# A fused recurrent-attention and MoE kernel: scalar loads further back on GpSimd, three loads split, and a new order of loads and work

## The chip, the cores and the metric

The kernel runs on one core of a Trainium2 chip. The metric is the time of one execution on the device in microseconds (us). The kernel before took 186.28 us, the median of 13 runs (184.48 to 188.73).

A core has five engines, each with an instruction queue of its own that runs in order: TensorE (PE, matrix products; its weight loads are listed as PEld), VectorE (DVE), ScalarE (ACT), GpSimd (POOL) and SyncE (SP, which here only issues DMAs). The queues meet at semaphores. An instruction that waits holds back all that stand behind it on its queue.

## The reference

Two parts follow each other. The first is a gated linear recurrence over 768 steps for 4 batches of 8 heads, with head size 48:

```python
for t in range(S):
    state = alpha[:, :, t, :, None] * state + np.einsum('bhd,bhe->bhde', k[:, :, t], v[:, :, t])
    y[:, :, t] = np.einsum('bhd,bhde->bhe', q[:, :, t], state)
```

Its output, put together to x of 3072 tokens by 384, goes through one layer with a hidden size of 2048:

```python
h = x @ w_in
r = np.maximum(h, 0.0)
g = s * (r * r) + b
return (g @ w_out).astype(np.float32)
```

The scalars s and b are single numbers. Inputs and output are float32.

## The kernel before

**Blocks.** The 3072 tokens are 24 blocks of 128 (6 to a batch). Within a block the recurrence is written as matrix products. ACT takes the logarithm of alpha (`st_ln`, L381); PE sums it over time with a triangular matrix (`st_cum`, L387, and L394 for the sum over the block); ACT takes the exponential of the sums and of their negatives (L403, L406, L408); DVE multiplies q and k with these (L417, L422); POOL casts v (L411). The scaled q and k are needed transposed: ACT issues a DMA transpose for that (`st_Tdma`, L439). PE then forms the key-value product for the state (L448) and the scores (`st_A`, L490), DVE masks the scores (L499) and updates the state (L469, L473; POOL L484 multiplies with the block's decay), PE forms y (L528), and ACT copies y to bf16 (L673).

**Pairs.** The first four blocks are loaded and worked two by two ("pairs" 0 and 1, L551 to L661), with PE in place of the DMA transposes (L605, copied out by DVE at L616). Half of a pair's values have to change their place among the partitions: POOL casts them (L621), PE moves them (`pair_vshift`, L631), and `pair_vcopy` (L644) copies them out of PSUM, on the engine that `VC2` names.

**The layer.** Finished blocks are put into groups of one or two (`GROUPS`, L18). For each group the first product is done in units of 512 output columns in PSUM (`mm1`, L693): six matmuls of 256 columns for a group of two blocks, twelve of 128 for a single one. There are 96 units. ACT applies the ReLU (L702) and DVE squares (L708). The second product (`mm2`, L755) is done in quads of four matmuls, four quads to a block; DVE scales it with s and adds the bias (L766), and SP stores it (L779). The bias row is b times the column sums of w_out: DVE adds these up (L343, L348, L351), multiplies ones with b (L363), and one matmul (L368) makes the row. The eight weight pieces, called i0 to i3 and o0 to o3, come in float32 and are cast to bf16 by the engines in `CE` (L319 on ACT, L321 on DVE, L323 on POOL).

**What sets the order.** A planner (class `Schedule`, L55 to L143) takes all operations with an engine, a cost, a priority and what they read and write. It runs through them with its own clock, gives each engine the ready operation of lowest priority value, and writes out the instructions in the order found. Priorities are a block's due time `want(n)` (from `UNIT` and `LEAD`) plus an offset for the kind of operation (the table `P`). Costs, such as `TC` for the casts, also only affect the order. Where the planner sees PE idle before the first `mm2`, it puts filler matmuls on zeros (L1028). The order of the first loads on SP is the list `LOADS`: capitals stand for pairs, small letters for single blocks. Later loads come in the order of their blocks, and a load waits until its one of five buffers is free. Stores stand on the same SP queue. One store, of block `STQ` = 18, is issued by POOL.

**Places that the change touches.** The scalar loads (`load_bs`, L358 to L360, planned at L847) stand on POOL behind the setup memsets and ahead of the first value casts of pair 0. `load` (L223 to L228) issues one DMA for one tensor of one block. `NKV` says from which block on the key-value product uses another PSUM bank, `NPE` up to which block PE would transpose a single block; since the first four blocks are pairs, that is none.

Of the kernel before, what the change touches and what calls it, by code (L numbers as in the profile page):

```python
# [14 lines left out]

VW = 144

GROUPS = [2, 2, 1, 1, 1, 1, 2, 2, 2, 2, 2, 2, 2, 2]  # L18
UNIT = 0.392
LEAD = {1: 204.6, 2: 323.1, 4: 100.0}  # L20

NPE = 4

NAY = 12

# [6 lines left out]
TP = 1.45  # L32
LATE = 2.5
NY = 2
NKV = 7
NR2 = 2
STQ = 18
TC2 = ["DVE", "DVE"]
VC2 = ["ACT", "ACT"]
CE = ["POOL", "DVE", "ACT", "ACT", "ACT", "ACT", "ACT", "ACT"]  # L40
TC = dict(ACT=1.4, DVE=0.87, POOL=2.0)
FILL_GAP = 0.2
COLD = 9.0

P_BM, P_CS, P_BMM = -5, -286.4, 473.5
P = dict(
    ln=34.88, cum=-15.29, eb=-32.24, ei=9.49, vc=73.43, qb=-9.65, kb=14.71, T=95.62,
    Tc=-13.62, KV=-13.54, t1=9.55, sn=124.73, Ay=-11.39, A=-22.53, mk=-58.68, y=-13.83,
    ye=5.65, m1=-19.67, re=9.86, sq=-33.02, m2=-18.25, oe=-24.3, vm=-57.17, ci=324.52,
    co=-825.8, ls=148.33, vn=-450.01,  # L50
)

LOADS = ["V0", "i0", "A0", "K0", "Q0", "A1", "V1", "Q1", "i1", "K1", "i2", "i3", "v4", "o0", "o1", "o2", "o3", "a4", "k4", "q4"]

class Schedule:  # L55
    HOP = 0.05
# [90 lines left out]
def kernel(  # L147
# [12 lines left out]
    nc = tc.nc  # L160
    ctx.enter_context(tc.manual_schedule())

    B, H, S, D = q.shape
    C = 128
# [7 lines left out]
    NIN = 5  # L172
# [31 lines left out]
    a_in = many("a_in", NIN, [128, H, D], FP32)  # L204
# [17 lines left out]

    def load(n, src, dst):  # L223
        b, c = n // NCH, n % NCH
        nc.sync.dma_start(
            out=dst[n % NIN],
            in_=src[b, :, c * C : (c + 1) * C, :].rearrange("h s d -> s h d"),
        )  # L228

    for x, src in enumerate((alpha, q, k, v)):  # L230
        load_pair(0, x, src)
# [62 lines left out]
    out_sb = many("o_sb", 3, [128, d_model], FP32)  # L294
# [368 lines left out]
    blk_group = []  # L663
    for g, m in enumerate(GROUPS):
        blk_group += [(g, t) for t in range(m)]
# [11 lines left out]
    quads = []  # L677
    for g, m in enumerate(GROUPS):
        per = 4 // m
        for u in range(NJ // per):  # L680
            units.append((g, [u * per + i for i in range(per)]))
        for tt in range(m):
            for jq in range(NJ // 4):
                quads.append((g, tt, jq))
    first_blk = [sum(GROUPS[:g]) for g in range(len(GROUPS))]

    def mm1(w):
        g, js = units[w]
        n = GROUPS[g] * C
        hp = h_ps[w % 2]  # L690
# [84 lines left out]
    def ostore(x):  # L775
        g, tt, jq = quads[x]
        n = first_blk[g] + tt
        eng = nc.gpsimd if n == STQ else nc.sync
        eng.dma_start(out=out[n * C : (n + 1) * C, :], in_=out_sb[(x // 4) % 3])  # L779


    sched = Schedule()
    op = sched.op
    NG = len(GROUPS)

# [31 lines left out]
    for rank, item in enumerate(loads):  # L817
        t, i = rank - 1000, int(item[1:])
        if item[0] in "AQKV":
            if i == 1:  # L820
                load_pair_op(item[0], i)
            continue
        if item[0] in "aqkv":
            if i < N1 + NIN:
                load_op(item[0], i)
            continue
        st = stage
        stage += 1
        key = [("wst", st)]
        if st >= NST:  # L830
            h = (st - NST) // 2 % 2
            key = [("gt", x, j) for x in range(9 - 3 * h, 12 - 3 * h) for j in range(NJ)]
            key = key[24 * (st % 2) : 24 * (st % 2) + 24] + [("wst", st)]
        if st >= NST:
            reuse.append((len(sched.ops), [(x, h) for x in ("AQ", "KV")[st % 2]]))
        eng = CE[st]
        if item[0] == "i":
            op("SP", TW, t, load_w_in, i, st, w=key, lat=2.0)
            op(eng, TC[eng], P["ci"], cast_w_in, i, st, eng, r=key, w=[("wib", i)], lock=eng != "ACT")
        else:  # L840
            op("SP", TW, t, load_w_out, i, st, w=key, lat=2.0)
            op(eng, TC[eng], P["co"], cast_w_out, i, st, eng, r=key, w=[("wob", i)], lock=eng != "ACT")
            op("DVE", 0.88, P_CS, colsum_part, i, st, r=key,
               w=["colpart" if i else "colsum"], lock=True)
            if i:
                op("DVE", 0.88, P_CS, colsum_add, r=["colpart"], w=["colsum"], lock=True)
    op("POOL", 1.3, P["ls"], load_bs, w=["b", "s"], lat=3.5)  # L847
    op("DVE", 0.3, P_BM, bias_mul, r=["b"], w=["bones"], lock=True)
    op("DVE", 0.44, P_CS, colsum_fold, w=["colsum"], lock=True)
    ys = {}  # L850
# [4 lines left out]
    def pb(n):  # L855
        return "ct" if n >= NKV else "py"

# [106 lines left out]
    def add_group(g):  # L964
        nonlocal unit_i, quad_i
        if g == 0:
            op("PE", 0.65, P_BMM, bias_mm, r=["bones", "colsum"], w=[("o", 0)], lat=0.16)
            op("DVE", 0.53, -300, bias_copy, r=[("o", 0)], w=["bias"])
        m = GROUPS[g]
        ring = [(first_blk[g] + x) % RING for x in range(m)]  # L970
        per = 4 // m
        for u in range(NJ // per):
            w = unit_i
            unit_i += 1
            js = units[w][1]
            t = w * UNIT
            op("PE", {1: 0.67, 2: 0.656, 4: 0.648}[m], t + P["m1"], mm1, w,
               r=[("xd", g % 3, x) for x in range(m)] + [("wib", js[0] // 4)],
               w=[("h", w % 2)], lat=0.16)
            op("ACT", 0.52, t + P["re"], relu, w, r=[("h", w % 2)], w=[("r", w % 2)])  # L980
            op("DVE", 0.345, t + P["sq"], square, w, r=[("r", w % 2)],
               w=[("gt", x, j) for j in js for x in ring], lock=True)
        for u in range(4 * m):
            x = quad_i
            quad_i += 1
            tt, jq = quads[x][1:]
            if x >= len(quads) - 4:
                continue
            ob = (x // 4) % 2
            t = (x + 4 * m + P["m2"]) * UNIT  # L990
            op("PE", 0.65, t, mm2, x,
               r=[("gt", ring[tt], j) for j in range(4 * jq, 4 * jq + 4)] + [("wob", jq)],
               w=[("o", ob)], lat=0.16)
# [69 lines left out]
```

## Time and profile before

| what | value |
|---|---|
| median of 13 runs | 186.28 us |
| the profiled execution: time, span in the profile | 186.5 us, 184.7 us |
| mean granted clock of PE | 0.982 |
| PE, PEld busy | 173.6, 123.8 us |
| DVE, ACT, POOL busy | 133.4, 105.7, 39.9 us |
| first products L693 | 73.2 us in 672 matmuls |
| second products L755 | 68.9 us in 368 matmuls |
| ReLU L702, square L708 | 55.3 and 42.4 us, 96 each |
| HBM read, written | 25.17 MB, 4.72 MB |
| DMA transposes, issue to landing | 20, 2.9 to 6.8 us, median 5.3 |
| loads of 192 KB, issue to landing | 4.7 to 4.8 us at the median |

The span runs from the first to the last instruction; the execution's time is 1.8 us longer. Busy times leave out the instructions that only issue DMAs, so an ACT that is issuing a transpose does not show as busy. Matmuls are pipelined, and their ends are modelled: their starts are the safer thing to read. The chain that ended last is found by going back from the last instruction, at each step to what released it; "issue" in it is time for which the profile shows no reason.

### The profile page before, as it was taken

The page shows a single profiled execution, that of the slowest core. Times are in us where ns is not written, and L with a number is a line of the kernel's source. Part 1 is how long each engine was busy: PE and PEld are TensorE (multiplying, and loading weights), DVE is VectorE, ACT ScalarE, POOL GpSimd, SP SyncE. Part 2 cuts the span into 40 slices and gives each one's busy share as a digit, 9 for nine tenths or more (in the row PEclk, how much of TensorE's full clock was granted, in tenths as well). Part 3 has the DMA queues.
Part 4 walks back from the last instruction along what each step waited for, and adds up shares of the span by engine and source line. Part 5 has one row for each costly group of instructions (what it writes and reads, how often), then busy time and mean ns, then how long its engine had stood idle before and what let it go on. Part 6 is the DMA issues. An engine that isn't in the chain of part 4 may idle for free.

```text
span 184.7 us, 5347 instructions
## 1 busy us (share of the span) xinstructions
PE 173.6 (94%) x2151; PEld 123.8 (67%) x2151; DVE 133.4 (72%) x251; ACT 105.7 (57%) x215; POOL 39.9 (22%) x71
## 2 busy tenths in 40 slices
PE   6689996999999999999989999999999799999993
PEld 2345774756778677766667776787767577777662
DVE  2477799999497887759769996878778586553321
ACT  3434899956646565685357674685657355665000
POOL 7994032021013311211203230111212130010000
PEclk9975999999999999999999999999999999999999
DMA  5999999999999999999999999999986892000122
GB/s 154 357 272 386 349 372 282 181 174 239 248 191 225 188 149 282 178 209 222 229 192 229 178 217 229 197 192 170 215 173 137 154 173 77 0 19 28 56 76 85
DMA packets 119961, 35.48 MB, mean 192 GB/s; under 512 B 113232, under 2 KB 118352, under 8 KB 119936
## 3 DMA queue, kind: packets, MB, share of 16 engines
q1 hardware_dynamic: 98688, 29.70, 70.9%
q10 hardware_dynamic: 21120, 5.25, 22.0%
q8 instruction: 17, 0.28, 0.6%
q0 software_dynamic: 128, 0.20, 0.3%
q14 instruction: 8, 0.07, 0.1%
HBM read 25.17 MB, written 4.72 MB: 162 GB/s over the span
## 4 chain that ended last, share of the span: by engine, by line
PE 64%; DVE 12%; DMA 10%; POOL 5%; issue 3%; ACT 3%; ACTq 1%; SPq 0%; POOLq 0%; DVEq 0%
PE o_ps L755 25%; PE h_ps L693 24%; DMA qkT<-qk 7%; PE py_ps L528 4%; PE a_ps L490 3%; DMA v_in<-in_v_dram 3%; DVE gt L708 2%; DVE colpart L343 2%; ACT r L702 2%; DVE colsum L348 2%; DVE am L499 2%; PE ct_ps L387 1%; DVE s_st L473 1%; PE o_ps L1028 1%; PE o_ps L724 1%
## 5 line engine op out<-in xcount | busy, mean ns | idle before, releaser
L693 PE MATMUL h_ps<-xd,w_in_bf 128*128 128x256 bf16 (+1 forms) x672 | 73.2, 257 | 0.7 <-ACT r L702 0.6
L702 ACT ACTIVATE r<-h_ps 128x512 bf16<-128x512 f32 x96 | 55.3, 601 | 29.7 <-PE h_ps L693 10.4
L755 PE MATMUL o_ps<-w_out_bf,gt 128*128 128x384 bf16 x368 | 68.9, 326 | 1.4 <-ACT w_out_bf L319 1.3
L693 PEld LDWEIGHTS <-w_in_bf 128*128 128x128 bf16 x672 | 56.2, 98 | 10.5 <-issue 1.0
L708 DVE TENSOR_TENSOR gt<-r 128x512 bf16<-128x512 bf16 x96 | 42.4, 456 | 15.2 <-ACT r L702 14.8
L755 PEld LDWEIGHTS <-gt 128*128 128x128 bf16 x368 | 34.3, 98 | 20.3 <-issue 1.5
L499 DVE TENSOR_TENSOR am<-a_ps,mask 128x1024 bf16<-128x1024 f32 x24 | 29.3, 1221 | 3.2 <-PE a_ps L490 3.0
L411 POOL CAST vp<-v_in 128x384 bf16<-128x384 f32 x20 | 12.0, 600 | 61.3 <-DMA v_in<-in_v_dram 48.4
L484 POOL TENSOR_TENSOR s_st<-s_st,blast 128x384 bf16<-128x384 bf16 x16 | 14.0, 874 | 49.0 <-DVE s_st L473 29.2
L766 DVE SCALAR_TENSOR_TENSOR o_sb<-o_ps,s_col,bias_w 128x384 f32<-128x384 f32 x23 | 14.2, 615 | 8.8 <-PE o_ps L755 8.4
L673 ACT ACTIVATE xd<-py_ps 128x384 bf16<-128x384 f32 x22 | 11.1, 504 | 11.9 <-PE py_ps L528 11.8
L381 ACT ACTIVATE la<-a_in 128x384 bf16<-128x384 f32 x20 | 10.5, 527 | 7.0 <-DMA a_in<-in_alpha_dram 3.5
L417 DVE TENSOR_TENSOR qk<-q_in,b_s 128x384 bf16<-128x384 f32 x20 | 11.9, 597 | 2.6 <-ACT b_s L403 2.5
L473 DVE TENSOR_TENSOR s_st<-ct_ps,s_st 64x192 bf16<-64x192 f32 x24 | 8.5, 354 | 6.5 <-PE ct_ps L448 5.4
L403 ACT ACTIVATE b_s<-ct_ps 128x384 f32<-128x384 f32 x20 | 9.8, 491 | 5.7 <-PE ct_ps L394 3.3
L422 DVE TENSOR_TENSOR qk<-k_in,binv 128x384 bf16<-128x384 f32 x20 | 11.0, 549 | 0.9 <-DMA k_in<-in_k_dram 0.8
L490 PEld LDWEIGHTS <-qkT 64*128 64x128 bf16 x192 | 5.6, 95 | 6.8 <-issue 5.1
L490 PE MATMUL a_ps<-qkT 64*128 64x128 bf16 x192 | 9.8, 222 | 0.4 <-DMA qkT<-qk 0.2
L406 ACT ACTIVATE binv<-ct_ps 128x384 f32<-128x384 f32 x20 | 9.9, 494 | 0.0
L1028 PE MATMUL o_ps<-zeros 128*128 128x512 bf16 x21 | 7.6, 495 | 1.3 <-DVE zeros L236 1.3
L528 PE MATMUL py_ps<-am,vp 128*32 128x128 bf16 x352 | 8.8, 219 | 0.0
L528 PEld LDWEIGHTS <-vp 128*32 128x32 bf16 x384 | 6.8, 100 | 0.5 <-issue 0.2
(93 smaller groups left out, 125.5 us busy)
## 6 DMA issues: line engine op xcount, KB each, us to landing
out_dram<-o_sb SPq DMA_DIRECT2D x22, 192.0 KB, 2.9
v_in<-in_v_dram SPq DMA_DIRECT2D x20, 192.0 KB, 4.8
a_in<-in_alpha_dram SPq DMA_DIRECT2D x20, 192.0 KB, 4.8
k_in<-in_k_dram SPq DMA_DIRECT2D x20, 192.0 KB, 4.7
q_in<-in_q_dram SPq DMA_DIRECT2D x20, 192.0 KB, 4.7
wst<-in_moe_w_in_dram SPq DMA_DIRECT2D x4, 768.0 KB, 8.0
gt<-in_moe_w_out_dram SPq DMA_DIRECT2D x4, 768.0 KB, 9.5
gt<-in_alpha_dram SPq DMA_DIRECT2D x2, 384.0 KB, 4.6
```

What stands on the lines that cost most here:

```text
L411: nc.gpsimd.tensor_copy(out=vp_sb[n % 4].rearrange("a p (x d) -> a p x d", d=D)[:, :, 0:3:2, :], in_=v_in[n % NIN].rearrange("a (p e) d -> ...
L417: nc.vector.tensor_tensor(out=qk_sb[n % 4][:, 0, :, 0:D], in0=q_in[n % NIN], in1=b_sb[n % 2], op=ALU.mult)
L484: nc.gpsimd.tensor_tensor(out=s_sb[n % 3], in0=t1_sb[n % 2], in1=bl, op=ALU.mult)
L490: nc.tensor.matmul(out=a_ps[:, e, p, :], lhsT=qkT[64 * e : 64 * e + 64, 1, p, :], rhs=qkT[64 * e : 64 * e + 64, 0, p, :], start=True, stop ...
L499: nc.vector.tensor_tensor(out=am_sb[n % 2].rearrange("a e p t -> a (e p) t"), in0=a_ps.rearrange("a e p t -> a (e p) t"), in1=(mask2 if n ...
L528: nc.tensor.matmul(out=y_of(n)[32 * (x % 4) : 32 * (x % 4) + 32, x // 4, :], lhsT=(st[:, p, c0 : c0 + 32] if e is None else vp[:, p, c0 + ...
L673: nc.scalar.activation(out=dst, in_=src, func=AF.Copy)
L693: nc.tensor.matmul(out=hp[:, i * n : (i + 1) * n], lhsT=w_in_bf[:, kk, 128 * j : 128 * (j + 1)], rhs=xd_sb[g % 3][:, kk, 0:n], start=(kk = ...
L702: nc.scalar.activation(out=r_sb[w % 2], in_=h_ps[w % 2], func=AF.Relu)
L708: nc.vector.tensor_tensor(out=gt_sb[:, s0 : s0 + m, js[0] : js[0] + len(js)].rearrange("a s j t -> a j s t"), in0=r, in1=r, op=ALU.mult,)
L755: nc.tensor.matmul(out=op[:, 0:d_model], lhsT=gt_sb[:, s0, j], rhs=w_out_bf[:, j, :], start=(j == 0), stop=(j == NJ - 1),)
L766: nc.vector.scalar_tensor_tensor(out=ots, in0=o_ps[(x // 4) % 2][:, 0:d_model], scalar=s_col, in1=bias_w, op0=ALU.mult, op1=ALU.add,)
```

## The change

Seven things change. The first is a new dependence, which makes the planner put the scalar loads behind the arrival of pair 1's values. The second splits three loads (q, k and v of block 20) into two DMAs of four heads each. Third, the store of block 18 goes to SP. Fourth, `VC2` puts one of the two value copies of each pair on DVE. Fifth, the groups change: nine of two blocks and six of one, instead of ten and four. Sixth, `LOADS` has a new order. Seventh, the planner gets other due times, offsets, costs and port rules, so that the order of the instructions changes on every engine. `NKV` goes from 7 to 6.

```diff
-GROUPS = [2, 2, 1, 1, 1, 1, 2, 2, 2, 2, 2, 2, 2, 2]
-UNIT = 0.392
-LEAD = {1: 204.6, 2: 323.1, 4: 100.0}
-NPE = 4
+GROUPS = [2, 1, 1, 1, 2, 2, 2, 1, 2, 2, 1, 2, 2, 1, 2]
+UNIT = 0.92
+LEAD = {1: 111.4, 2: 111.7, 4: 19.2}
+NPE = 3
...
-NKV = 7
+NKV = 6
-STQ = 18
-VC2 = ["ACT", "ACT"]
+VC2 = ["DVE", "ACT"]
-TC = dict(ACT=1.4, DVE=0.87, POOL=2.0)
+TC = dict(ACT=1.43, DVE=1.7, POOL=1.44)
...
-LOADS = ["V0", "i0", "A0", "K0", "Q0", "A1", "V1", "Q1", "i1", "K1", "i2", "i3", "v4", "o0", "o1", "o2", "o3", "a4", "k4", "q4"]
+LOADS = ["i0", "A0", "V0", "A1", "V1", "i1", "K0", "Q0", "Q1", "K1", "v4", "i2", "i3", "o0", "o1", "q4", "o2", "o3", "a4", "k4"]
...
     def load(n, src, dst):
         b, c = n // NCH, n % NCH
-        nc.sync.dma_start(
-            out=dst[n % NIN],
-            in_=src[b, :, c * C : (c + 1) * C, :].rearrange("h s d -> s h d"),
-        )
+        parts = 2 if n == 20 and dst is not a_in else 1
+        for x in range(parts):
+            hs = slice(H // parts * x, H // parts * (x + 1))
+            nc.sync.dma_start(
+                out=dst[n % NIN][:, hs],
+                in_=src[b, hs, c * C : (c + 1) * C, :].rearrange("h s d -> s h d"),
+            )
...
-        eng = nc.gpsimd if n == STQ else nc.sync
-        eng.dma_start(out=out[n * C : (n + 1) * C, :], in_=out_sb[(x // 4) % 3])
+        nc.sync.dma_start(out=out[n * C : (n + 1) * C, :], in_=out_sb[(x // 4) % 3])
...
-    op("POOL", 1.3, P["ls"], load_bs, w=["b", "s"], lat=3.5)
+    op("POOL", 1.3, P["ls"], load_bs, r=[("V", 1)], w=["b", "s"], lat=3.5)
```

All entries of `P` change as well (for the scalar loads, ls goes from 148.33 to 233.89), and the casts of weights and two costs of matmuls in the planner. How the order comes out: on POOL the two scalar loads stand behind pair 1's casts and the state update of block 1, and ahead of block 4's value cast; before, they were the first thing behind the memsets. On DVE the value copies stand behind pair 0's copies of transposes (L616) and behind block 1's mask, and the bias multiply L363 moves from behind block 1's mask to behind pair 1's copies of transposes. On PE there are 51 matmuls more: 48 of the first product and three fillers. On SP the store of block 15, which stood ahead of block 22's k and v loads, stands behind all loads.

More of the change, by code (lines that the diff above doesn't have):

```diff
@@ L34 @@
 NY = 2
-NKV = 7
+NKV = 6
 NR2 = 2
-STQ = 18
 TC2 = ["DVE", "DVE"]
-VC2 = ["ACT", "ACT"]
+VC2 = ["DVE", "ACT"]
 CE = ["POOL", "DVE", "ACT", "ACT", "ACT", "ACT", "ACT", "ACT"]
-TC = dict(ACT=1.4, DVE=0.87, POOL=2.0)
+TC = dict(ACT=1.43, DVE=1.7, POOL=1.44)
 FILL_GAP = 0.2
 COLD = 9.0
-P_BM, P_CS, P_BMM = -5, -286.4, 473.5
+P_BM, P_CS, P_BMM = -5, -217.4, 512.0
 P = dict(
[L47 to L50, printed above, removed]
+    ln=50.93, cum=-11.7, eb=-25.98, ei=-14.28, vc=58.17, qb=19.99, kb=-17.0, T=38.45,
+    Tc=-30.89, KV=-13.93, t1=-24.57, sn=118.3, Ay=-40.59, A=-32.64, mk=-45.84, y=-19.88,
+    ye=10.8, m1=-10.02, re=0.24, sq=-21.45, m2=-8.17, oe=-41.19, vm=-66.4, ci=345.81,
+    co=-1666.27, ls=233.89, vn=70.38,
 )
-LOADS = ["V0", "i0", "A0", "K0", "Q0", "A1", "V1", "Q1", "i1", "K1", "i2", "i3", "v4", "o0", "o1", "o2", "o3", "a4", "k4", "q4"]
+LOADS = ["i0", "A0", "V0", "A1", "V1", "i1", "K0", "Q0", "Q1", "K1", "v4", "i2", "i3", "o0", "o1", "q4", "o2", "o3", "a4", "k4"]
 class Schedule:
@@ L838 @@
             op("SP", TW, t, load_w_in, i, st, w=key, lat=2.0)
-            op(eng, TC[eng], P["ci"], cast_w_in, i, st, eng, r=key, w=[("wib", i)], lock=eng != "ACT")
+            op(eng, TC[eng], P["ci"], cast_w_in, i, st, eng, r=key, w=[("wib", i)], lock=eng == "POOL")
         else:
             op("SP", TW, t, load_w_out, i, st, w=key, lat=2.0)
-            op(eng, TC[eng], P["co"], cast_w_out, i, st, eng, r=key, w=[("wob", i)], lock=eng != "ACT")
+            op(eng, TC[eng], P["co"], cast_w_out, i, st, eng, r=key, w=[("wob", i)], lock=eng == "POOL")
             op("DVE", 0.88, P_CS, colsum_part, i, st, r=key,
@@ L976, in add_group @@
             t = w * UNIT
-            op("PE", {1: 0.67, 2: 0.656, 4: 0.648}[m], t + P["m1"], mm1, w,
+            op("PE", {1: 0.675, 2: 0.66, 4: 0.652}[m], t + P["m1"], mm1, w,
                r=[("xd", g % 3, x) for x in range(m)] + [("wib", js[0] // 4)],
@@ L990, in add_group @@
             t = (x + 4 * m + P["m2"]) * UNIT
-            op("PE", 0.65, t, mm2, x,
+            op("PE", 0.655, t, mm2, x,
                r=[("gt", ring[tt], j) for j in range(4 * jq, 4 * jq + 4)] + [("wob", jq)],
```

## The prediction

> **What bounds the kernel now.** I read the page first (shares of the span, the 40 slices), then the windows by stage, then the chain that ended last, then the waits, and the timeline only where these pointed.
>
> ```profile
> span 184.7 us, 5347 instructions
> ...
> PE 173.6 (94%) x2151; PEld 123.8 (67%) x2151; DVE 133.4 (72%) x251; ACT 105.7 (57%) x215; POOL 39.9 (22%) x71
> ...
> PEclk9975999999999999999999999999999999999999
> ```
>
> TensorE is busy nearly throughout, and the only half-speed stretch lies in slices 2 and 3 (about 9 to 18.5 us). The windows view splits this into stages:
>
> ```profile
> 10.00:15.00 5.00, 4.31 (x49) 2.11 (x52) 3.34 (x8) 1.70 (x3) 4.64 (x8) 0.68 1.08 297
> ...
> 30.00:35.00 5.00, 4.15 (x52) 3.29 (x41) 4.97 (x8) 5.00 (x6) 0.78 (x1) 1.00 0.86 180
> ...
> 40.00:50.00 10.00, 10.00 (x125) 6.68 (x124) 7.43 (x16) 6.61 (x16) 1.47 (x2) 1.00 1.24 229
> ```
>
> The columns after the length are PE, PEld, DVE, ACT, POOL busy, then clock and DMA. There are three stages. Up to 19.5 us a latency chain runs through POOL, PE and DVE. From 19.5 to 38 us DVE (18.03 of 18.50 busy) and ACT (17.77) are full, and the bias matmul at 38.04 waits for DVE's column sums. From 38 us on PE is full. So time can be won in three ways only: an earlier start of the second stage, a shorter second stage, or fewer stalls of PE in the third.
>
> The chain shows where the first stage hangs:
>
> ```profile
> 8.21 0.63 POOL b_col L359
> 8.84 0.54 POOL s_col L360
> 9.38 0.52 POOL vc L621
> ...
> 10.52 0.51 POOL vp L621
> 11.07 0.41 PE py_ps L655 x6
> 11.70 0.35 DVE s_st L469
> ```
>
> The two scalar loads stand on POOL ahead of the value casts, and these ahead of the first key-value matmuls. The values had landed at 7.81 (their issue at 3.00 plus 4.81), so the loads hold the chain.
>
> In the third stage the same view shows the largest stall:
>
> ```profile
> 139.38 0.63 DVE o_sb L766
> ...
> 140.02 0.36 SPq L779
> ...
> 140.43 0.43 SPq L225
> ...
> 140.95 5.00 DMA v_in<-in_v_dram
> ...
> 146.07 0.51 POOL vp L411
> ...
> 146.63 0.33 PE ct_ps L448 x4
> ```
>
> A store on SP waits for its output tile; behind it stand block 22's k and v loads; the value lands 5.00 us after its issue, is cast, and PE has stood 1.09 us (start of the matmul less start and usual 0.16 us of the one before). Measured in this way, starts against usual starts, the stalls over 0.2 us after 40 us are 0.21 at 61.4, 0.36 at 70.4, 0.80 at 96.3, 0.26 at 108.4 and 1.09 at 146.6: 2.7 us in all. Two are named in the waits:
>
> ```profile
> PE ct_ps L448 <- POOL vp L411: 0.9, 1, 0.9
> PE h_ps L693 <- ACT r L702: 0.6, 1, 0.6
> ```
>
> **Part by part.** Line numbers are those of before.
>
> *Scalar loads (L359, L360) behind the second pair's values.* POOL's first cast starts at 8.21 instead of 9.38, so 1.17 us earlier. What is late next? The two pair transposes on PE end at 9.77, so the first shift matmul gains little (9.94 to about 9.8), the second goes from 10.51 to about 10.0, and the first key-value matmuls from 11.07 to about 10.2, when the third cast is done. Then DVE is late: its second copy of transposes ends at 10.65 either way, and the change puts a value copy there (L644, 0.49 on ACT), so the state operation starts at about 11.15 instead of 11.70. The mask follows at 11.9 (was 12.47), the next score matmuls at 13.5 (were 14.21), the first y at 14.05 (14.76). One more filler matmul ahead of the second y costs 0.43 at half clock, of which about 0.15 shows; y starts at 15.5 (16.08), and the pair's scaling on DVE, which opens the full stretch, at about 19.0 instead of 19.53. Gain: 0.55. The floor is 0, if DVE or the fillers eat it; the ceiling 1.17.
>
> *The loads' new place.* They issue after the first state update, at about 14.6 instead of 8.16, and landed 4.3 us later at the longest, so at about 19. The bias multiply (L363, 0.28) moves from a gap at 16.01 to behind the pair's transposes, at about 23. That hides the landing with 4 us to spare. But its 0.28 now lies in the full DVE stretch: a loss of 0.28. The Trainium skill, page "SBUF — State Buffer", section "SBUF: two separate sides", speaks against this place: a DMA issued by GpSimd cannot have its descriptors written while VectorE holds the shared port, and the next section tells of 620 ns grown to 3100 ns. By that page I estimate two such delays, 5 us, and then a stall of about 1 us at the bias multiply and a sum 1 us worse; no row here shows it, since both loads ran while VectorE had gaps.
>
> *Value copies on DVE, one per pair.* Both fall where DVE waited (1.05 before 11.70, 1.30 before 19.53); the first is in the chain above, the second costs nothing.
>
> *Load order.* i1 goes ahead of Q1, v4 ahead of i2, q4 ahead of o2. Transfers land one behind the other here (192 KB in 0.5 to 0.9 us), so o3 lands at about 33.0 instead of 32.41. Its first user on DVE ran at 35.24; even 0.5 earlier it is covered by 1.7. Nothing.
>
> *Groups.* Nine groups of two blocks and six of one replace ten and four. One pair of blocks more is done by 96 matmuls of 128 columns instead of 48 of 256. Twelve of the first kind take as long as six of the second: the chain has 24 of the first kind in 1.34 at 48.14 and 12 of the second in 1.33 at 81.06. Eight units at 0.01: 0.1 loss.
>
> *Three late loads (q, k, v of block 20) split in two.* Three more issues on SP, 0.4 to 0.8 each. SP stands still from 126.4 to 127.95 just behind them. Nothing, at most 0.3.
>
> *Store of block 18 from POOL to SP.* SP then does it among the last stores; nothing waits behind it but stores. Nothing.
>
> *New order of SP.* I counted PE's work (0.665 a unit of first matmuls, 0.65 a quad of second ones, 0.34 scores, 0.56 y) between the end of the block whose store stands just ahead of a load and that load's use. Before, the shortest are k22 3.5 us, k7 5.5, k11 5.7, k15 6.2; after, k7 7.0, a22 7.4, k14 8.0. A load took 4.7 to 4.8 at the median from issue to landing. So the stall at 146.6 goes (1.09), and so does the one at 108.4 (0.26), whose k15 was scaled 0.7 late for that reason. What is late next there is a22: 7.4 us against about 6 needed. Gain 1.35; bounds 0.7 to 1.4.
>
> *New order of PE, ACT and DVE.* Three distances matter. First, from a block's cumulative sum to its scores lie exponentials, scaling and a DMA transpose of 2.9 to 6.8 us (median 5.3). It gets shorter in 14 of 20 blocks: 13.1 to 10.9 for block 7, 9.9 to 8.4 for 11, 8.8 to 8.0 for 8, 8.2 to 7.5 for 23. With the transposes of before, block 9 stalls 0.3 again and 5, 7, 13 come within 0.7 of it; I put 0.6 against the 0.36 of before: loss 0.25. Second, the stall at 96.3 is ACT's: a transpose issue held it 2.18 instead of 1.27, and the next first matmul had 0.5 us to spare. The shortest such reserve is 0.67 after, and three were under it before: gain 0.5 of the 0.8. Third, DVE: between a first matmul and the one that needs its buffer again stand a ReLU (0.60), a square (0.46) and what DVE has queued ahead; in two units (29 and 60) 0.2 us are left over there, where none had under 0.8: loss 0.4, up to 1.
>
> Sum: -0.55 + 0.28 + 0.1 - 1.35 + 0.25 - 0.5 + 0.4 = -1.4. The profiled execution took 186.5 (its span and 1.8 around it), which is 0.2 over the median 186.28. So 185.1 in its terms and **184.9** in those of the median.
>
> **Rivals.** *The stalls only move (186.1).* The load stalls end, but PE is full, and the tighter transposes and squares take it back: 0.55 gained, 0.38 lost (0.28 + 0.1), and 1.85 (1.35 and 0.5) offset by 1.8. For it: DVE works 15 to 17 of each 20 us in the third stage and convoys move easily. Against: the load stalls have a named cause that goes. This is also the case in which the change does not do what it says, since the scalar loads' own part is then worth 0.2.
>
> *The transposes become the bound, on the other side (188.1).* If each takes 1 us longer than before, because the loads that now stand ahead of the stores share the DMA engines with them, blocks 4 to 16 have -0.3 (5), -0.7 (7), -0.2 (8), -1.3 (9), -0.4 (11), -0.6 (13), -0.3 (16) to spare: a loss of 3.8 in place of 0.6, so 3.2 over the forecast, 188.1. The point from which it costs more than the rest gains is about 0.45 us more per transpose (1.4 of 3.2), a mean of 5.5 instead of 5.1. For it: a spread of 2.9 to 6.8 already. Against: the bytes are the same.
>
> *The clock (183.5 or 188.3).* The half-speed stretch is 6.83 us long (11.79 to 18.62). Without it the first stage's PE pieces, about 3 us in the chain, would halve: 1.4 faster. A second one would cost up to 3.4. Nothing in the change aims at it.
>
> **Numbers.** Forecast 0.52, stalls only move 0.23, transposes 0.15, a faster clock or all the first 1.17 us kept 0.10. The forecast's own range is 183.9 to 185.8 (the start 0.6 either way, SP's 0.65, squares 0.6, not all at once). The whole range reaches to the others: 183.1 to 187.4. A measurement here can tell 0.5%, 0.93 us, from no change: faster means under 185.35, slower over 187.21. The forecast lies 0.45 under the first bound, so about a quarter of its cases fall within 0.5%. Faster: 0.39 of the forecast's 0.52, 0.08 of the second case and the last 0.10, 0.57; slower: 0.13 of the transposes' and 0.04 of the second case, 0.17; the rest, 0.26, is no change.
>
> **What would show it.** In the chain of after, POOL's casts at 8.2 and the first pair of key-value matmuls before 10.5; the bias matmul at 37.4 to 37.9; the bias multiply not waiting for its scalar; no wait of PE on the value cast late; transposes at a median of 5.3; squares waited for near units 29 and 60. Wrong: the bias matmul at 38 or later, or PE waiting over 1.5 us in all on transposed tiles.

## The result and the profile after

The changed kernel took 188.66 us (median of 11 runs, 188.01 to 190.19). The kernel before took 186.09 (median of 48 runs, 183.46 to 188.73). The ratio is 1.019, with a 95% interval of 1.016 to 1.022: slower by 3.5 us, where 1.4 us faster was forecast, and above the forecast's range. This ratio and all that follow compare fast runs alone, those within 1.5% of a kernel's fastest (here 11 of 11, and 27 of the 48 of before), since executions also come in a slower state; so the 3.5 us exceed the 2.6 us between the medians of all runs.

The profiled execution took 189.05 us. From the page of the changed kernel, the lines that answer to those of before:

```profile
span 187.3 us, 5473 instructions
...
PE 172.5 (92%) x2202; PEld 123.4 (66%) x2202; DVE 133.5 (71%) x253; ACT 105.3 (56%) x213; POOL 39.2 (21%) x70
```

The span is 2.6 us longer and every engine is as busy as before, so waiting was added and not work. TensorE ran at full clock throughout in this execution, while that of before had 6.8 us at half clock; the early stage of the two can therefore not be compared piece by piece. Pair 1's scaling, which opens the second stage, starts at 17.80 instead of 19.53. The bias matmul, the border of the second and third stage, starts at 40.56 instead of 38.04; from there to the end it is 146.78 us instead of 146.66. **So between these two executions the whole loss lies in the second stage, 22.76 us long instead of 18.51, and the third has gained nothing.**

The windows of after (PE, PEld, DVE, ACT, POOL busy, clock, DMA share, GB/s; the share adds up the times of all packets and can come to over 1):

```profile
20.00:25.00 5.00, 3.83 (x48) 2.87 (x45) 2.48 (x6) 2.56 (x3) 0.65 (x1) 1.00 0.55 182
25.00:30.00 5.00, 2.52 (x49) 2.07 (x49) 4.62 (x8) 3.62 (x4) 0.99 (x1) 1.00 1.09 368
```

The first of these stretches in the windows of before:

```profile
20.00:25.00 5.00, 4.93 (x57) 3.74 (x56) 4.75 (x8) 4.46 (x8) 0.50 (x1) 1.00 1.09 347
```

Between 20 and 25 us the DMA engines moved 182 GB/s instead of 347, though the weights were queued. Such a stretch is called a hole below. DVE, which was to be full, worked 2.48 of 5 us. Five us later the DMAs are back, but PE has half a stretch of work.

The chain of after shows what hung on what:

```profile
15.83 0.77 POOL s_st L486
16.60 7.73 DMA b_col<-in_moe_b_dram
...
24.42 0.06 DVE bones L365
...
26.63 1.00 POOL s_st L486
...
42.39 5.59 DMA v_in<-in_v_dram
...
48.10 0.51 POOL vp L413
...
48.65 0.33 PE ct_ps L450 x4
```

The load of b, 0.5 KB, was issued at 16.60 and took 7.73 us to land; before, it was issued at 8.16 and took 4.29. The last three lines are a new stall: the value of block 6 lands at 47.98 (44.87 before), and PE stands 1.56 us before the product that needs it. DVE's row in the timeline of after gives the wait for b, in the brackets at its end:

```profile
24.42 0.29 DVE L365 TENSOR_SCALAR bones<-ones_f,b_col 128x128 f32<-128x128 f32 x1 [2.48 <-DMA b_col<-in_moe_b_dram]
```

The weights landed late too: i3 at 26.36 (23.19 before), o3 at 36.60 (32.41).

### The profile page after: what moved, and what is told of

Read it like the earlier page. It is cut to its first block, busy times and chain, and to the rows that moved or that the text cites. A ratio compares the mean times of both kernels' runs of the same rounds, so it can differ in the third digit from the quotient of the medians.

```text
span 187.3 us, 5473 instructions
## 1 busy us (share of the span) xinstructions
PE 172.5 (92%) x2202; PEld 123.4 (66%) x2202; DVE 133.5 (71%) x253; ACT 105.3 (56%) x213; POOL 39.2 (21%) x70
## 4 chain that ended last, share of the span: by engine, by line
PE 64%; DMA 13%; SPq 8%; DVE 6%; ACT 3%; issue 3%; POOL 2%; POOLq 0%; ACTq 0%; DVEq 0%
PE o_ps L757 25%; PE h_ps L695 25%; SPq L227 7%; PE py_ps L530 4%; DMA b_col<-in_moe_b_dram 4%; DMA qkT<-qk 4%; PE a_ps L492 3%; DMA v_in<-in_v_dram 3%; DVE am L501 2%; DMA gt<-in_alpha_dram 2%; PE ct_ps L450 2%; ACT r L704 1%; PE ct_ps L389 1%; DVE s_st L475 1%; POOL s_st L486 1%
## 5 line engine op out<-in xcount | busy, mean ns | idle before, releaser
L695 PE MATMUL h_ps<-xd,w_in_bf 128*128 128x256 bf16 (+1 forms) x720 | 75.6, 251 | 2.7 <-ACT r L704 1.3
L704 ACT ACTIVATE r<-h_ps 128x512 bf16<-128x512 f32 x96 | 56.2, 601 | 36.1 <-PE h_ps L695 20.0
L757 PE MATMUL o_ps<-w_out_bf,gt 128*128 128x384 bf16 x368 | 70.6, 326 | 1.9 <-ACT w_out_bf L321 1.9
L695 PEld LDWEIGHTS <-w_in_bf 128*128 128x128 bf16 x720 | 57.4, 98 | 13.4 <-ACT w_in_bf L321 2.3
L710 DVE TENSOR_TENSOR gt<-r 128x512 bf16<-128x512 bf16 x96 | 41.3, 448 | 20.9 <-ACT r L704 20.4
L413 POOL CAST vp<-v_in 128x384 bf16<-128x384 f32 x20 | 11.3, 563 | 42.2 <-DMA v_in<-in_v_dram 29.8
L530 PE MATMUL py_ps<-qkT,s_st 128*32 128x128 bf16 x228 | 6.7, 222 | 0.2 <-DVE s_st L475 0.2
## 6 DMA issues: line engine op xcount, KB each, us to landing
gt<-in_moe_w_out_dram SPq DMA_DIRECT2D x4, 768.0 KB, 11.5
```

The source lines that it names most:

```text
L413: nc.gpsimd.tensor_copy(out=vp_sb[n % 4].rearrange("a p (x d) -> a p x d", d=D)[:, :, 0:3:2, :], in_=v_in[n % NIN].rearrange("a (p e) d -> ...
L530: nc.tensor.matmul(out=y_of(n)[32 * (x % 4) : 32 * (x % 4) + 32, x // 4, :], lhsT=(st[:, p, c0 : c0 + 32] if e is None else vp[:, p, c0 + ...
L695: nc.tensor.matmul(out=hp[:, i * n : (i + 1) * n], lhsT=w_in_bf[:, kk, 128 * j : 128 * (j + 1)], rhs=xd_sb[g % 3][:, kk, 0:n], start=(kk = ...
L704: nc.scalar.activation(out=r_sb[w % 2], in_=h_ps[w % 2], func=AF.Relu)
L710: nc.vector.tensor_tensor(out=gt_sb[:, s0 : s0 + m, js[0] : js[0] + len(js)].rearrange("a s j t -> a j s t"), in0=r, in1=r, op=ALU.mult,)
L757: nc.tensor.matmul(out=op[:, 0:d_model], lhsT=gt_sb[:, s0, j], rhs=w_out_bf[:, j, :], start=(j == 0), stop=(j == NJ - 1),)
```

## The experiments

Three theories stood at the start. **T1**: the late scalar loads hold up the other transfers while they are moved. **T2**: what costs is only DVE's wait for b. **T3**: the new order of the big loads on SP costs the time. Ratios in this section are to the kernel before, timed on the same chip, with 95% intervals. The table gives for each kernel when o3 landed, when the bias matmul began, and the DMA share in the windows from 20 to 25 us.

| kernel | o3 lands | bias matmul | DMA 20 to 25 | ratio |
|---|---|---|---|---|
| before | 32.41 | 38.04 | 1.09 | 1 |
| after | 36.60 | 40.56 | 0.55 | 1.019 [1.016, 1.022] |
| e1 scalars early | 35.44 | 39.38 | 0.90 | 1.009 [1.005, 1.012] |
| e2 early, and late ones unread | 36.22 | 41.33 | 0.87 | 1.013 [1.004, 1.022] |
| e3 scalars by ACT | 36.45 | 40.41 | 0.98 | 1.015 [1.006, 1.024] |
| e4 before, scalars late | 33.39 | 37.69 | 0.74 | 1.005 [1.000, 1.009] |
| e5 early, old load order | 32.34 | 37.88 | 1.08 | 1.001 [0.997, 1.005] |
| e6 late, old load order | 33.27 | 38.10 | 0.82 | 1.005 [1.000, 1.010] |
| e7 product of block 6 later | 35.90 | 39.96 | 0.68 | 1.016 [1.008, 1.023] |
| e8 multiply late | 35.81 | 40.61 | 0.60 | 1.013 [1.010, 1.017] |
| e9 no scalars | 34.00 | 37.99 | 1.03 | 1.002 [0.997, 1.006] |
| e10 scalars by SP, old loads | 32.44 | 37.08 | 0.82 | 1.002 [0.998, 1.005] |
| e11 e10, product two quads later | 34.00 | 39.15 | 0.87 | 0.999 [0.995, 1.003] |
| e12 before, scalars by SP | 32.93 | 37.39 | 0.77 | 0.998 [0.994, 1.001] |
| e13 one element each, unread | 34.04 | 38.08 | 0.95 | 1.006 [1.002, 1.010] |
| e14 128 pieces each, unread | 35.81 | 40.27 | 0.73 | 1.016 [1.011, 1.021] |
| e15 no scalars, old loads | 32.37 | 37.40 | 1.08 | 0.997 [0.994, 1.000] |
| e16 one element, spread | 33.34 | 38.50 | 1.07 | 0.994 [0.990, 0.999] |
| e17 before, one element, spread | 31.90 | 37.60 | 1.09 | 0.995 [0.990, 1.000] |
| e18 e16 again | 31.64 | 36.79 | 1.09 | 0.999 [0.994, 1.003] |

A warning on how to read it: e10 and e11 are the same up to 40 us, and yet their bias matmuls lie 2.07 us apart. The profiled executions also differ in their clock: TensorE's granted clock was half from about 11.5 to 18 us in e1, from 26 to 29.5 in e2, from 28.5 to 35.5 in e8 and from 25.5 to 32 in e14, and the bias matmuls of these four may be late in part for that. A single profile shows how a delay comes about; its size is taken from the ratios. Where two ratios are subtracted, the interval of the difference is given; the chips of the two can differ.

**e1**, the scalar loads put back to the front of GpSimd's queue, all else as in after:

```diff
+    load_bs()
...
-    op("POOL", 1.3, P["ls"], load_bs, r=[("V", 1)], w=["b", "s"], lat=3.5)
+    op("POOL", 1.3, P["ls"], lambda: None, r=[("V", 1)], w=["b", "s"], lat=3.5)
```

> The changed kernel with one part undone: the two scalar loads stand on GpSimd where they stood before, behind the memsets and ahead of the first value casts; every other order is that of after. Theory T1 (the late scalar loads hold up the other transfers: from 21 to 25 us of after only 5.5 to 8 of 16 DMA engines are at work, where before it is 17 by the same count): the hole goes, the bias matmul comes back from 40.6 to 37.5 to 38.3, the stall of 1.56 us at block 6's value goes too, and the time is 184.7 to 186. Theory T2 (only VectorE's wait of 2.48 us for the scalar b costs time): 186 to 186.5, and the hole in the transfers stays, since it has another cause. Theory T3 (the new order of the big loads costs the time): 188 to 188.7.

1.009: half of the 1.9% goes, and half stays. So the late place costs, and something beside it does.

**e2**, as e1, and two more loads of 0.5 KB at the late place, read by nobody:

```diff
+    def load_idle():
+        nc.gpsimd.dma_start(out=idle_b, in_=moe_b.to_broadcast((128, 1)))
+        nc.gpsimd.dma_start(out=idle_s, in_=moe_s.to_broadcast((128, 1)))
```

> The kernel of e1 with two more loads: b and s are loaded a second time into tiles that nobody reads, at the place where the changed kernel has its scalar loads. Nothing waits for them. T1: they hold up the other transfers all the same, i3 and the pieces behind it land 2 to 4 us later than in e1, and the time is 1.5 to 3 us over e1. T2: as e1, within 0.5 us. T3: as e1.

1.013, not told apart from e1 by the intervals; the DMA share falls to 0.76 from 15 to 20 us, and the bias matmul is later by 1.95 though nobody waits for these loads (part of it may be the clock). It leans to T1; e14 decides.

**e3**, the scalar loads issued by ACT at the start:

```diff
-        nc.gpsimd.dma_start(out=b_col, in_=moe_b.to_broadcast((128, 1)))
+        nc.scalar.dma_start(out=b_col, in_=moe_b.to_broadcast((128, 1)))
```

> The changed kernel with the two scalar loads issued by ScalarE's queue at the start, where ScalarE waits for the first alpha; GpSimd issues none. T1, if the disturbance belongs to loads that GpSimd issues late: no hole in the transfers, and the 1.2 us that GpSimd spends on issuing are saved as well: 0 to 0.7 us under e1, 184.3 to 186. If small transfers of 4 bytes a partition disturb the others from any queue: a hole early on, and the first alpha lands later by 0.5 us or more, 186 or over. T2: 184.3 to 186. T3: 188.

1.015, no cure: ahead of everything, they made the first alpha land 1.2 us later (5.35 instead of 4.16) and the first values 1.9 us (9.82 instead of 7.93).

**e4**, the kernel before, with only the scalar loads and the multiply moved to their late places:

```diff
         nc.gpsimd.tensor_tensor(out=s_sb[n % 3], in0=t1_sb[n % 2], in1=bl, op=ALU.mult)
+        if n == 1:
+            load_bs()
```

> The kernel before with that one part of the change: the scalar loads behind the state update of block 1 on GpSimd, the bias multiply behind pair 1's copies of transposes on VectorE, nothing else. T1: the hole in the transfers appears here too, between about 21 and 26 us, and the time is 188 to 190. T2: the multiply waits 0.5 to 2 us for b, 186.7 to 188, with the transfers full. T3: 186 to 186.5, since the order of the big loads is that of before.

1.005. b landed at 21.53, and DVE had no wait for it at 22.80. In the old order of loads the same move costs 0.5% (0.0 to 0.9), where the loads cost 1.75% in the new one (e9 below).

**e5 and e6**, the three loads that had moved ahead on SP put back (i1 behind Q1, v4 behind i3, q4 behind k4), with the scalars early (e5) and late (e6). That gives the order of the first loads of before, since pair 0's four loads are issued ahead of the list `LOADS` in both kernels:

```diff
+    sched.moves = [("i1", "Q1"), ("v4", "i3"), ("q4", "k4")]
```

> The changed kernel with two parts undone: scalar loads at the start of GpSimd's queue, and three loads on SP back in the places of before (i1 behind the first pair's q load, v of block 4 behind i3, q of block 4 behind k of block 4); all other orders as in the changed kernel. With e1, e6 and the changed kernel this makes four kernels, scalars early or late by load order new or old. T3 (the new order of loads costs what the scalars do not: pulling v4 and q4 ahead fills the queue of descriptors in flight, SP issues the weights later, and o3 and v of block 6 land 2 to 4 us later): i3 lands at about 23.5, o3 at about 32.5, v of block 6 at about 45, the bias matmul at about 37.5 instead of 39.4, the stall ahead of block 6's key-value product goes, time 184.5 to 186, under the kernel before. Rival (load order is nothing, as forecast): time as e1, 187.5, bias matmul at about 39.4.

> The changed kernel, its scalar loads where it puts them (late), with the same three loads on SP back in the places of before. T1 and T3 (late scalars and load order both cost, and add up): 186 to 187.5, bias matmul at about 38.5 to 39.5, a hole in the hardware queue's packets at 21 to 25 us all the same. T1 alone: time as the changed kernel, 188.7. T3 alone: as e5.

The load order is worth 0.8% (0.2 to 1.3) with early scalars (e1 to e5) and 1.4% (0.9 to 1.9) with late ones (after to e6); T1 and T3 both seemed to hold. But the stall at block 6's product stayed (1.25 us in e5), and no version beat the kernel before.

**e7**, block 6's product moved on PE:

```diff
+    sched.moves = [("st_KV6", "st_y6")]
```

> The changed kernel, with the key-value product of block 6 on PE moved from 2.6 us behind its cumulative sum to behind the y of block 6, some 2.4 us of PE's work later; all loads as in the changed kernel. If the early place of this product on PE turns late loads into a stall, the 1.56 us at 48.6 go and the time is 187.1 to 187.6. Rival (the value's lateness is paid anyhow, by the state of block 6 being late for block 7): PE stalls as long a little later, 188.5.

The edit moved more than was meant: in its trace the product runs at 57.19, 8.5 us later than in after, and not 2.4. At 1.016 it is level with after; the stall at 48.6 went, 1.00 us of waiting for a square at 48.0 and later waits for transposes came. It says nothing on a small move; e11 does.

**e8**, the bias multiply moved behind the last fold of the column sums:

```diff
+    sched.moves = [("bias_mul", "colsum_fold")]
```

> The changed kernel, loads as they are, with the bias multiply on DVE moved from behind the second pair's copies of transposes to behind the last fold of the column sums, so that DVE doesn't stand 2.48 us for b. T2 (DVE's wait is the cost): bias matmul at 38.1 to 38.6 instead of 40.56, time about 186.5. T1 (the late scalar loads hold up the other transfers, and DVE's wait hides behind that): the weights land as late as before, DVE waits for them instead, bias matmul at 39.5 to 40.5, time 187.8 to 188.7.

1.013: 0.6% better than after (the intervals put it between 0.1 and 1.1), with the bias matmul as late as ever, which may in part be the clock. So T2 has a small part.

**e9**, after without the scalar loads (0.5 and 1.0 stand for b and s):

```diff
+    nc.gpsimd.memset(b_col, 0.5)
+    nc.gpsimd.memset(s_col, 1.0)
```

> The changed kernel without its two scalar loads: GpSimd writes 0.5 and 1.0 into the two tiles during setup, so b and s are not the inputs'. All orders and all other loads as in the changed kernel. If the holes in the hardware queue (5 to 8 of 17 engines' worth of packets at 21 to 25 us in the changed kernel, 5.9 at 12 us in e1) are the scalar loads' doing, there is none here before 30 us, o3 lands at 34 to 34.5 (its place in the new load order costs the rest of 32.41 to 36.60), bias matmul at about 38.5, time 186.5 to 187. If the new load order makes the holes by itself, they stay, o3 lands at 35.5 or later, time as e1: about 0.9% over the kernel before.

**1.002, level with the kernel before.** So the two loads cost 1.75% (1.25 to 2.25; 1.019 less 1.0015), 3.3 us, all of the loss within the interval. Its windows:

```profile
20.00:25.00 5.00, 4.64 (x85) 3.51 (x81) 4.83 (x10) 4.18 (x5) 0.90 (x2) 1.00 1.03 352
```

352 GB/s and 4.83 us of DVE, with the same order of loads as in after, where it was 182 and 2.48. o3 lands 2.6 us earlier.

**e14**, as e9, with two loads of 0.5 KB into 128 partitions at the late place, read by nobody; **e13**, the same two loads, of one element into one partition (both with 0.5 and 1.0 for b and s):

```diff
+        nc.gpsimd.dma_start(out=idle_b, in_=moe_b.to_broadcast((128, 1)))
+        nc.gpsimd.dma_start(out=idle_s, in_=moe_s.to_broadcast((128, 1)))
```

In e13 both have `(1, 1)` in place of `(128, 1)`.

> As e13, but the two unread loads on GpSimd go to 128 partitions, as those of the changed kernel do: the hole alone, with no wait of DVE for b. With e9 and the changed kernel it divides the 1.75% between the hole and the wait. T1 (the hole): 1.2 to 1.8% over the kernel before, packets at 5 to 8 of 17 engines for 3 to 4 us. T2 (the wait): 0.2 to 0.5%.

> The changed kernel's orders, no b and s from the inputs (0.5 and 1.0 written during setup, as in e9), and at the place of the late scalar loads on GpSimd two loads of one element each, one partition instead of 128, that nobody reads. If the hole comes from the 128 tiny pieces that a load into 128 partitions falls into, it is gone: time as e9, 0.0 to 0.4% over the kernel before. If any DMA issued by GpSimd at this place makes it (its descriptors are late, whatever their number), packets fall under 10 of 17 engines at 20 to 25 us and the time is over 1% up.

e14 is at 1.016, with nobody waiting for its loads; e13 is at 1.006. From the windows of e14:

```profile
15.00:20.00 5.00, 4.88 (x69) 3.58 (x61) 4.94 (x7) 3.17 (x7) 2.82 (x4) 1.00 0.69 189
20.00:25.00 5.00, 3.10 (x41) 2.32 (x39) 4.26 (x9) 2.56 (x3) 0.82 (x1) 1.00 0.73 268
```

From those of e13:

```profile
20.00:25.00 5.00, 4.70 (x83) 3.39 (x79) 4.89 (x11) 3.10 (x4) 0.80 (x1) 1.00 0.95 313
```

In e14 the hole is there (189 and 268 GB/s) with no wait for b: it costs 1.4% (0.8 to 2.1) over e9, most of what after loses, and T2 is left with 0.3 to 0.6%. The half clock does not explain it: e14's six runs took 188.05 to 190.35, and the two whose mean granted clock was 1.000 and 0.999 took 190.19 and 188.51. With one element in place of 128 pieces most of the hole is gone, and 1.0% (0.3 to 1.6) with it; what is left, 0.5% over e9, the intervals do not tell from nothing.

**e15**, e9 (0.5 and 1.0 for b and s) with the three loads put back as in e5:

```diff
+    sched.moves = [("i1", "Q1"), ("v4", "i3"), ("q4", "k4")]
```

> As e9 (no scalar loads, 0.5 and 1.0 written during setup), with the three loads on SP back in the places of before. With e9 it prices the new load order without scalar loads: T3 as first stated (the new order costs by itself) puts it 0.8% or more under e9; if the order costs only by making the scalar loads' hole worse, it is within 0.4% of e9.

0.997 against 1.002: without scalar loads the new load order costs 0.4% (-0.1 to 1.0), not told apart from nothing, nor quite from the 0.8% that T3 asked for. With the late loads it costs 1.4% (after to e6), 1.0% more (0.2 to 1.7): that part it costs only together with them. With the early ones the excess, 0.3%, is not shown.

**e10** and **e12**, the scalars issued by SP behind i3 and the multiply behind the last fold, in after's order with the old load places (e10) and in the kernel before (e12):

```diff
         def load_w_in(i, st):
...
+        if i == 3:
+            load_bs()
```

> The changed kernel with the three loads back in the places of before, the scalar loads issued by SP behind i3 in place of GpSimd, and the bias multiply behind the last fold of the column sums. No DMA is issued by GpSimd in the first 35 us. T1 with T3: no hole in the hardware queue, GpSimd's casts early, pair 1's scaling at 18.0 to 18.9, o3 lands at 32.5 to 33, bias matmul at 37.0 to 37.6 (0.4 to 1.0 before that of the kernel before), stall at block 6's key-value product 1.2 to 1.5; 0.3 to 0.5% under e5 and the kernel before, the first of these kernels to be faster. Rival (the small loads delay a queue that they stand in, as on ScalarE's in e3): o3 at 33.5 or later, time as e6, 0.5% over the kernel before.

> The kernel before, and only the scalar loads moved: SP issues them behind i3, and the bias multiply stands behind the last fold of the column sums. The first part of the forecast by itself, without GpSimd's DMA: GpSimd's casts 1.2 us earlier, pair 1's scaling at 18.6 to 19.0 instead of 19.53, bias matmul at 37.2 to 37.6 instead of 38.04, time 0.2 to 0.5% under the kernel before. Rival (the weights' landing sets the second stage, not the chain through GpSimd): bias matmul at 38.0 all the same, time as before.

Both are level with before, short of what T1 hoped for. From the windows of e12:

```profile
20.00:25.00 5.00, 4.93 (x90) 3.86 (x89) 4.68 (x10) 4.34 (x6) 0.90 (x2) 1.00 0.77 241
```

Issued by SP, the 128 pieces bring the rate down to 241 GB/s just as well, and the first part's gain (bias matmul 0.65 earlier in e12, beside an execution of before that was in part at half clock) may be paid back in part; that is not shown. GpSimd's issuing is thus not needed for the hole.

**e11**, e10 with block 6's product behind the next two quads of second products:

```diff
+    sched.moves = [("i1", "Q1"), ("v4", "i3"), ("q4", "k4"), ("bias_mul", "colsum_fold"), ("st_KV6", "mm28")]
```

> As e10, and block 6's key-value product on PE stands behind the next two quads of second products (1.5 us of PE's work later, still ahead of block 4's y). If its early place costs the stall, 1.2 to 1.5 us go in the third stage, time 0.6 to 0.8% under e10. Rival (third-stage stalls only move, as when it was moved behind block 6's y in e7): the same stalls come back on transposed tiles and squares, time within 0.3% of e10.

0.999 against 1.002, not told apart. The stall at the product (1.87 in e10) is gone, 0.91 of waiting for a square at 47.05 came.

**e16** and, as **e18**, once more: e11's orders, the scalars loaded late by GpSimd as one element each and spread over the 128 partitions by a matmul with ones and a copy:

```diff
+        nc.gpsimd.dma_start(out=bs_one[:, 0:1], in_=moe_b.to_broadcast((1, 1)))
+        nc.gpsimd.dma_start(out=bs_one[:, 1:2], in_=moe_s.to_broadcast((1, 1)))
...
+        nc.tensor.matmul(
+            out=o_ps[0][:, 0:2], lhsT=ones_f[0:1, :], rhs=bs_one, start=True, stop=True
+        )
+        nc.vector.tensor_copy(out=bs_col, in_=o_ps[0][:, 0:2])
```

> A whole kernel again, from what the runs point to: the changed kernel with the three loads back in the places of before, block 6's key-value product two quads later, the scalars loaded late by GpSimd as one element each, spread over 128 partitions by one matmul with ones (behind the first product of unit 6) and a copy on DVE, and the bias multiply behind the last fold. If the tiny pieces are the cost: no hole, bias matmul at 37.0 to 37.6, time 0.4 to 0.9% under the kernel before. If a GpSimd DMA costs by itself, as e11 or worse.

> The kernel of e16 once more, on the same chip as e17, because its interval ended just under 1 while the medians of all its runs and of the kernel before were level (186.39 and 186.31). If it is faster, 0.3 to 0.9% under the kernel before again, and level with e17 or better by 0.3%; if the first result was luck, within 0.3% of the kernel before.

0.994 and 0.999; the medians of all runs are 186.39 beside 186.31, and 186.69 beside 185.90. No hole (1.07 and 1.09), but it is not shown to be faster than before. (The profiled execution of e16, 186.68 us, lies near the top of its runs, 183.87 to 187.34.)

**e17**, the kernel before with e4's late place, and e16's one element each (matmul, copy and the multiply's place behind the last fold included):

```diff
-        nc.gpsimd.dma_start(out=b_col, in_=moe_b.to_broadcast((128, 1)))
+        nc.gpsimd.dma_start(out=bs_one[:, 0:1], in_=moe_b.to_broadcast((1, 1)))
```

> The kernel before with its scalar loads late on GpSimd, at the place of e4, but as one element each, spread by a matmul and a copy as in e16; the bias multiply behind the last fold. Against e4 (128 pieces at the same place: 0.5% over the kernel before) it prices the pieces in the old order: if they are the cost, 0.3 to 0.6% under the kernel before, no hole at 20 to 24 us, bias matmul at 37.1 to 37.6. If the place on GpSimd is the cost, as e4.

0.995 against e4's 1.005: 1.0% (0.3 to 1.6) for one element in place of 128 pieces, loaded at the same place. The multiply stands elsewhere than in e4, but there it had no wait and takes 0.28 us, 0.15%. From the windows of e4:

```profile
20.00:25.00 5.00, 4.37 (x59) 3.27 (x57) 4.96 (x11) 3.29 (x4) 0.00 (x0) 1.00 0.74 240
```

and of e17:

```profile
20.00:25.00 5.00, 4.40 (x64) 3.28 (x65) 4.79 (x10) 3.93 (x5) 0.51 (x1) 1.00 1.09 364
```

240 GB/s against 364. The load into 128 partitions is the cost in the old order of loads too. e17 (median 185.51 beside 185.90) lies at the edge of what the interval can tell from no change.

## Why the prediction was wrong

**The scalar loads' new place: the step that failed.** The sum had +0.28 for it; measured is 3.3 us (1.75%, e9). The prediction put the landing "at about 19" and found it hidden "with 4 us to spare". The issue came at 16.60 instead of 14.6, the landing took 7.73 us instead of 4.3, so that it fell at 24.33, and DVE waited 2.48. The larger mistake was to price these loads by who waits for them alone. They cost 1.4% with nobody waiting (e14 less e9), since while they are moved the big loads of the weights slow down (in after to 121 to 160 GB/s from 21 to 25 us). Of the prediction's two signs of being wrong, the first came: the bias matmul at 40.56. The trace of before already had a hint, for a reader who looks at it microsecond by microsecond. The early scalar loads' packets moved from 11.4 to 12.4 us:

```profile
10.00:11.00 1.00, 0.58 (x2) 0.14 (x2) 0.65 (x2) 0.14 (x1) 0.94 (x2) 1.00 1.17 325
...
12.00:13.00 1.00, 0.80 (x8) 0.51 (x8) 0.94 (x3) 0.59 (x1) 1.00 (x1) 0.50 0.70 140
```

At 12 us, 140 GB/s were moved instead of 325.

The page's estimate, which the prediction set aside, came nearer to DVE's wait than its rows did, but its reason is not borne out as the cause. In after the first packet of the scalar loads moved 5.0 us after their issue (21.62 after 16.60), against 3.25 in before, and DVE was busy until 21.94. But in e14 and e13, where DVE was busy without a gap from the issue on, the first packet came 2.56 and 1.31 us after it, and in e4, where DVE stood idle for 1.30 us of the time, 4.03. And in after DVE stood idle from 21.94 to 24.42, waiting for b, while the packets still trickled until 25.22. The Trainium skill, page "SBUF — State Buffer", section "SBUF: two separate sides", says that such a load, issued from ScalarE's or SP's queue, runs at full speed beside VectorE. No run here shows that, since on SP's queue the loads stood behind the weights (in e10 they landed at 22.57 and 22.75, just behind i3 at 22.40); and the harm to the other transfers stays with SP as the issuer (241 GB/s in e12).

**The early chain: right in its first steps, and not the chain that sets the second stage's start.** GpSimd's first cast starts at 8.26 (8.21 forecast), the first key-value matmuls at 10.51 (10.2). The state operation starts at 11.41 instead of 11.70, a gain of 0.29 where 0.55 was forecast: DVE's value copy ahead of it waited for ACT's, which ended at 10.79. e6 and e5 differ by the scalars' place alone, both at full clock: pair 1's scaling starts at 18.94 and 19.55, 0.61 apart. That this is near the forecast's 0.55 is luck. The scaling stands directly behind DVE's cast of i1, and for i1 DVE had waited, in e5 (the first line) and in e6 (the second):

```profile
17.88 1.75 DVE L331 CAST w_in_bf<-wst 128x1536 bf16<-128x1536 f32 x1 [0.86 <-DMA wst<-in_moe_w_in_dram]
...
17.27 1.75 DVE L331 CAST w_in_bf<-wst 128x1536 bf16<-128x1536 f32 x1 [0.44 <-DMA wst<-in_moe_w_in_dram]
```

i1 landed at 17.85 and 17.25. The prediction had no term for this landing. In after, with i1 ahead of Q1, it landed at 15.53, DVE had no wait for it, and the scaling started at 17.80, 1.2 us earlier than the 19.0 forecast.

**Load order: "nothing" holds only alone.** Without scalar loads, o3 lands at 34.00 (33.0 forecast) and the order costs some 0.4%, not told from nothing (e9, e15). With 128-piece loads it costs 0.8 to 1.4% (e5, e6). That two edits could make each other worse was in no term of the sum. Why they do is open. With early scalars the rate fell at 12 us to 83 GB/s in the new order (e1); in the old one it fell to 140 in before, but stayed at 285 or more in e5 while these loads were moved. So the depth of the hole also varies where the order of loads and the scalars' place are the same.

**The third stage: "the stalls only move".** The stalls forecast to go went: none is left at 146.6, 108.4 or 96.3 in the trace of after. The terms behind the bias matmul summed to -1.1 (0.1 - 1.35 + 0.25 - 0.5 + 0.4); measured is +0.12. PE's stalls over 0.2 us behind 40 us come to 3.2 us, against 2.7 before. The largest, 1.56 at 48.65, was overlooked: only loads behind stores were counted, while the value of block 6 is one of the first stream, and its product stands 2.6 us of PE's work behind its cumulative sum instead of 11.6. Next is 0.88 at 92.69, on a transpose of 7.08 us. So this sum is the second step that failed: it priced stalls that went and only some of those that came. What taking the largest away would gain is open, since e11, without it, is not told from e10. e9, the change without the scalars' harm, is at 1.002 (0.997 to 1.006), which leaves out the forecast's 184.9 (0.993) and holds the first rival's 186.1 (0.999). Transposes as a bound were not seen (median 4.7 us, 5.3 forecast), nor waits of PE behind squares near units 29 and 60.

**The small terms.** Value copies, groups, split loads and the store of block 18 were not tried singly; e9 holds them all, and together with the rest they come to 0.2% (-0.3 to 0.6).

**What stays open.** Why 128 pieces of 4 bytes hold up the weights' packets was not found. e13 and e17 change the number of pieces, of partitions and of reads of one address at once, and don't tell these apart. The traces don't either: on SP's queue e10 lists 288 more packets of 4 bytes than e9, 144 for each of the two loads; on GpSimd's queue such a load is listed as 16 packets of 32 bytes and 16 of 4, and the load of one element as 32 of 4, so that the count of packets listed there is the same.

## What to carry to other kernels

A load is not priced by its bytes and by who waits for it: look at what the other queues move while it is under way, microsecond by microsecond. A scalar that is to stand in all partitions was better loaded once and spread on the chip than read into 128 partitions, here by 1.0% where it was loaded among the big loads that bound a stage (e17 against e4). When a stage is as full as the third one here, count stalls that go only after looking for the next one at every consumer, not only where the queue's order changed.

## What the runs showed of the hardware

Two loads of 0.5 KB, in 128 pieces each and issued late, took the DMA rate of the 5 us from 20 to 25 us from some 350 to between 182 and 268 GB/s, on GpSimd's queue (after, e4, e6, e14) and on SP's (e10, e12) alike; on ScalarE's, ahead of all else, they made the first big loads 1.2 to 1.9 us late (e3). The same two as single elements left 313 to 364 GB/s (e13, e16, e17, e18). And two kernels that are the same up to 40 us (e10 and e11) differed by 2.07 us at the end of their load-bound stage.
